# Two of batch 0's key products on GpSimd behind the weights' issues, K in two loads, query products on GpSimd, and a new order list

## The chip, the cores and the metric

The kernel runs on one core of a Trainium2 chip. The metric is the device time of one execution in microseconds. Engines: PE is TensorE (matmuls), DVE is VectorE, ACT is ScalarE, POOL is GpSimd and SP is SyncE, which here issues DMAs only. All times are in microseconds unless ns is written.

## What is computed

A polynomial linear attention, followed by a two-layer feed-forward with SiLU. With 4 batches, 4 heads, 1088 rows and head size 32, r = 8:

```python
def phi(x):                      # 64 features of a row
    a = einsum('rd,bhsd->bhsr', S1, x)
    b = einsum('rd,bhsd->bhsr', S2, x)
    return einsum('bhsi,bhsj->bhsij', a, b).reshape(..., r * r)
q_p, k_p = phi(q), phi(k)
kv  = einsum('bhsf,bhsd->bhfd', k_p, v)
z   = sum(k_p, axis=2)
num = einsum('bhsf,bhfd->bhsd', q_p, kv)
den = einsum('bhsf,bhf->bhs', q_p, z)[..., None] + 1e-06
x   = (num / den).transpose(0, 2, 1, 3).reshape(4352, 128)
h   = x @ w_in                   # 128 x 2048
out = (h * sigmoid(h)) @ w_out   # 2048 x 128
```

## The kernel before, in words

The program is a set of small task functions, and a hand-written list, `ORDER` (lines 19 to 83), that names them one after the other with their arguments. A loop at the end (lines 601 to 604) calls them in that order. Each engine executes its own instructions strictly in the order in which the list recorded them; between engines there are semaphores where data or buffers demand it. So the list decides which instruction stands behind which on each engine, and a wait holds up all that is behind it.

For each batch b the attention goes through these tasks:

- `ld`, `lv` (lines 286 to 291) load K, Q and V. K and Q go through SP's queue, V of batches 1 to 3 through POOL's, which also casts it to bf16. Batch 0's loads stand by themselves at lines 188 to 201: K in four pieces, the second of them issued by ACT, the others by SP.
- `kt`, `qt` (lines 295 and 396): DVE transposes K and Q in blocks of 32.
- `pk` (line 299): PE projects K with the small weights WK into PSUM; `tk` (line 310): DVE transposes the result into the tile `pk` in SBUF. `pc` (line 326) has ACT copy one factor of it into PSUM as well.
- `zs`, `zc`, `mm`, `mk`: the sum of the key features, made into a weight column of WQ with which the denominator comes out of the query projection.
- `kp b e h` (line 319): one of four key products of a batch, 128 x 576 elements, on DVE or (P) on POOL. Where `pc` exists, DVE takes one factor from PSUM.
- `kv` (line 353): PE multiplies the key products with V. Batches 1 to 3 then need `km`, `kr`, `kw`, which mix heads with the constants `E4` and `same`; batch 0 needs only `kw`. The constants are made on POOL by `same_const` (line 270).
- `pq`, `tq`: query projection on PE and its transpose on DVE into `PQ`; `dn` (line 434): four short DVE instructions that apply the denominator (lines 437 to 440); `qo` (line 442): the query product; `pt`: its transpose into `qT`.
- `nm` (line 460): the numerator on PE, and `xc` copies it as bf16 into `xT`, the input of the feed-forward.

The feed-forward runs over 10 chunks of rows (`CHUNKS`), the first of 256, 384 and 448 rows, most others of 512. For each chunk, `f1 c s` makes two or four of the 16 hidden blocks (line 525), `sl c s` is SiLU on ACT (line 533), `f2 c s` adds the block to the output (line 557, or 552 for the last chunks) and `ot c` takes the result out. Three double PSUM banks (slots 0, 1 and 2, the last argument of `f1`, `pk`, `pq` and `nm`) are shared by the hidden blocks and the attention's products, so each must have been read before its slot is written again. The output tile of `f2` has one bank, shared with `zeros`, PE products of ones that are written and never read.

The letters A, V and P in the list choose the engine: ACT, DVE or POOL.

Of the kernel before, what the change touches and what calls it, by code (L numbers as in the profile page):

```python
# [31 lines left out]
dn 0 5 9, f1 1 2 0, tk 1, ld 3, f1 1 1 2, sl 1 0  # L32
lv 1, f2 0 3, f1 1 6 1, sl 1 2, zs 1, sl 1 1
lv 2, qo 0 5 9, sl 1 6, pt 0 5 9, f1 1 3 0, zc 1 V
lv 3, kp 1 1 0 P, sl 1 3, f1 1 5 2, ot 0, mm 1
sl 1 5, f2 1 0, kt 2 0 34, f1 1 7 1, f2 1 1, qt 1 0 34
nm 0 5 9 0, pk 2 2, sl 1 7, mk 1 V, kp 1 0 0 P, kp 1 1 1 P
tk 2, f2 1 2, xc 0 5 9 0 A, kp 1 0 1 P, pq 1 0 9 1 0, f1 2 0 2
kv 1, sl 2 0, tq 1 0 9 0, tq 1 0 9 1, f1 1 4 1, kp 2 1 0 P
f2 1 3, sl 1 4, f1 2 4 2, km 1 V, f1 2 5 0, dn 1 0 4  # L40
qo 1 0 4, f2 1 4, kr 1, kw 1 V, f2 1 5, sl 2 4
f1 2 1 1, pt 1 0 4, f1 2 2 2, sl 2 5, f2 1 6, f2 1 7
ot 1, f1 2 7 0, zs 2, sl 2 1, sl 2 2, dn 1 4 9
nm 1 0 4 1 2, xc 1 0 4 1 V, kt 3 0 34, sl 2 7, qo 1 4 9, f2 2 0
f1 2 3 0, xc 1 0 4 0 A, f2 2 1, f1 2 6 1, f2 2 2, sl 2 3
f1 3 2 2, sl 2 6, pt 1 4 9, f1 3 1 0, zc 2 V, f2 2 3
sl 3 2, f2 2 4, f1 3 0 1, pk 3 2, sl 3 1, tk 3
f1 3 5 0, qt 2 0 34, mm 2, mk 2 V, sl 3 0, f2 2 5
sl 3 5, nm 1 4 9 1 2, xc 1 4 9 0 A, f2 2 6, xc 1 4 9 1 A, f1 3 4 0
f2 2 7, pq 2 0 9 1 2, zs 3, sl 3 4, f1 3 6 0, ot 2  # L50
tq 2 0 9 1, f2 3 0, f1 3 3 2, tq 2 0 9 0, sl 3 6, zc 3 V
f1 4 0 1, dn 2 0 9, kp 2 0 1, sl 3 3, f2 3 1, f1 4 1 0
f2 3 2, qo 2 0 9, sl 4 0, kp 3 1 1 P, kp 2 0 0 P, sl 4 1
kp 2 1 1 P, f1 4 5 2, sl 4 5, f2 3 3, f1 3 7 1, kv 2
sl 3 7, f1 4 7 0, f2 3 4, km 2 V, f1 4 3 2, sl 4 7
f2 3 5, f1 4 6 1, kr 2, f1 4 2 0, pt 2 0 9, kw 2 V
f2 3 6, sl 4 3, sl 4 2, f2 3 7, mm 3, ot 3
mk 3 V, nm 2 0 9 2 0, f2 4 0, sl 4 6, f1 4 4 1, f2 4 1
xc 2 0 9 1 V, qt 3 0 34, xc 2 0 9 0 A, f1 5 0 2, kp 3 0 1, f2 4 2
f1 5 4 0, sl 4 4, f1 5 3 1, f2 4 3, sl 5 0, sl 5 4  # L60
sl 5 3, f2 4 4, pq 3 0 9 2 0, f2 4 5, kp 3 0 0, f1 5 1 1
kp 3 1 0, tq 3 0 9 0, f2 4 6, f1 5 2 2, tq 3 0 9 1, sl 5 1
f2 4 7, ot 4, f1 5 5 0, sl 5 2, sl 5 5, f1 5 6 1
kv 3, f1 5 7 2, f1 6 3 0, f2 5 0, sl 5 6, sl 5 7
f1 6 1 1, dn 3 0 9, f2 5 1, f2 5 2, f2 5 3, f1 6 6 2
km 3 V, sl 6 3, qo 3 0 9, f2 5 4, kr 3, sl 6 1
sl 6 6, f1 6 0 0, pt 3 0 9, f2 5 5, f1 6 2 1, f2 5 6
f2 5 7, sl 6 0, f1 6 4 2, sl 6 2, kw 3 V, ot 5
nm 3 0 9 0 1, f2 6 0, xc 3 0 9 1 V, sl 6 4, f1 6 7 2, f2 6 1
sl 6 7, xc 3 0 9 0 V, f1 6 5 1, f2 6 2, f1 7 1 2, f1 7 0 0  # L70
sl 6 5, f2 6 3, sl 7 1, f2 6 4, sl 7 0, f1 7 6 1
sl 7 6, f1 7 4 2, f2 6 5, f2 6 6, f1 7 3 0, f2 6 7
sl 7 4, sl 7 3, f1 7 2 1, f1 8 2 2, f1 7 5 0, ot 6
f2 7 0, sl 7 2, f2 7 1, f2 7 2, sl 8 2, f1 8 0 1
sl 7 5, f2 7 3, f1 7 7 2, f2 7 4, sl 8 0, f1 8 1 0
sl 7 7, f1 8 3 1, f2 7 5, f2 7 6, f2 7 7, ot 7
sl 8 1, f1 8 4 2, sl 8 3, f1 9 0 0, sl 8 4, f2 8 0
f1 8 5 1, f2 8 1, f1 9 3 2, sl 9 0, sl 8 5, f2 8 2
sl 9 3, f1 8 6 0, f2 8 3, f2 8 4, f1 8 7 1, sl 8 6
f1 9 1 2, f2 8 5, sl 8 7, f2 8 6, sl 9 1, f1 9 2 0  # L80
f1 9 4 1, sl 9 2, f2 8 7, f2 9 0 2, f2 9 1, sl 9 4
ot 8 V, f2 9 2, f2 9 3, f2 9 4, ot 9 V
"""


# [7 lines left out]
def kernel(  # L93
# [188 lines left out]

    def wo():
        nc.gpsimd.dma_start(w_out_bf, moe_w_out.rearrange("(p j) m -> p j m", p=P))
# [25 lines left out]
    def tk(b):  # L310
        t["pk", b] = work.tile([P, NC, 2, 2, 2, R], FP32, name="pk", tag="pk")

        kp_ = work.tile([P, NC * 8 * R * 4], BF16, name="kp", tag="kp")
        t["kp", b] = (kp_.rearrange("p (e n r h j i) -> p e n r h j i", e=2, n=NC, r=2, h=2, j=R) if b in HEADS
                      else kp_.rearrange("p (n r e h j i) -> p e n r h j i", e=2, n=NC, r=2, h=2, j=R))
        t["mark"] = nc.vector.transpose(out=t["pk", b].rearrange("p n r h a i -> p r n (h a i)"),  # L316
                            in_=t["pk_ps", b][:, :, :NC * 32].rearrange("p r (n f) -> p r n f", f=32))

    def kp(b, e, h, eng=nc.vector):
        s = t["pk", b][:, :, :, h].rearrange("p n r a i -> p (n r) a i")  # L320
        o = t["kp", b][:, e, :, :, h].rearrange("p n r j i -> p (n r) j i")
# [1 line left out]
        eng.tensor_tensor(out=o, in0=bcast(s[:, :, 0, 4 * e: 4 * e + 4], 2, R),  # L323
                          in1=bcast(s1, 3, 4), op=ALU.mult)

# [5 lines left out]
    def zs(b):  # L331
        t["z", b] = psA.tile([P, 2 * R], FP32, name="z_ps", tag="ac")
        for n in range(NC):
# [105 lines left out]
        nc.vector.reciprocal(out=dg, in_=dg)  # L439
        nc.vector.tensor_tensor(out=fa, in0=fa, in1=bcast(dg, 2, R), op=ALU.mult)  # L440

    def qo(b, q0, q1):
        fa, fb, fw = feats(b, q0, q1)
        if ("qp", b) not in t:
# [2 lines left out]
        nc.vector.tensor_tensor(out=t["qp", b][:, q0:q1].rearrange("p y h j i -> p (y h) j i"),  # L447
                                in0=bcast(fa, 2, R), in1=bcast(fb, 3, R), op=ALU.mult)
# [186 lines left out]
```

## Time and profile before

| what | value |
|---|---|
| time, three runs | 94.09, 94.91 and 97.61, median 94.91 |
| profiled execution | 93.98, of which 92.3 is the span |
| granted TensorE clock, mean | 0.996 |
| PE busy | 85.9 (93% of the span) |
| DVE busy | 61.3 (66%) |
| ACT busy | 70.6 (77%) |
| POOL busy | 25.0 (27%) |
| first expert product (`f1 0 0`) on PE | 15.39 by the order in time, 15.44 on the chain |

Busy time is the sum over an engine's instructions; the chain of work that ended last is followed backwards from the last instruction, at each step to what released it. A wait is put down to the instruction that came last before it ended.

### The profile page before, as it was taken

To read this page: it belongs to the slowest core of one execution; us is meant where nothing else is said; L and a number is where in the kernel's file an instruction comes from. 1 tells how busy PE (TensorE), PEld (TensorE's weight loads), DVE (VectorE), ACT (ScalarE), POOL (GpSimd) and SP (SyncE) were. 2 spreads that over 40 slices of the span, in tenths; PEclk is the share of its full clock that TensorE was granted. 3 is DMA by queue.
4 is the path that set the end of the run, shared out by engine and by line. 5 is a ranking of instruction groups with operands and counts; after the bars stand their busy time and mean duration, and the time that the engine had idled before them with its cause. 6 is when DMAs were issued, how large, how long until landed. Compare 5 with 4: busy or idle time off the path is not lost.

```text
span 92.3 us, 2484 instructions
## 1 busy us (share of the span) xinstructions
PE 85.9 (93%) x1006; PEld 52.7 (57%) x1006; DVE 61.3 (66%) x109; ACT 70.6 (77%) x88; POOL 25.0 (27%) x66
## 2 busy tenths in 40 slices
...
GB/s 33 248 234 220 158 210 319 321 248 322 269 351 144 5 50 36 7 0 80 26 4 0 60 54 7 11 102 0 0 54 60 7 64 49 0 57 43 7 79 96
DMA packets 20204, 9.31 MB, mean 101 GB/s; under 512 B 16096, under 2 KB 19040, under 8 KB 20192
## 3 DMA queue, kind: packets, MB, share of 16 engines
...
q10 hardware_dynamic: 448, 0.23, 1.0%
q8 instruction: 8, 0.13, 0.6%
...
## 4 chain that ended last, share of the span: by engine, by line
PE 86%; POOL 5%; ACT 3%; DVE 1%; issue 1%; POOLq 0%
PE h_ps L525 33%; PE o_ps L557 27%; PE o_ps L552 6%; PE pk_ps L306 5%; PE zps L249 4%; PE pq_ps L416 2%; ACT g L533 2%; PE kv_ps L365 2%; PE num_ps L476 2%; PE num_ps L467 2%; PE z_ps L337 1%; POOL same L277 1%; PE kv_ps L358 1%; POOL kp L323 1%; DVE pk L316 1%
## 5 line engine op out<-in xcount | busy, mean ns | idle before, releaser
L533 ACT ACTIVATE g<-h_ps 128x1024 bf16<-128x1024 f32 (+3 forms) x73 | 64.2, 1000 | 5.9 <-PE h_ps L525 5.4
L525 PE MATMUL h_ps<-xT,w_in_bf 128*128 128x512 bf16 (+3 forms) x160 | 38.8, 350 | 0.0
L557 PE MATMUL o_ps<-g,w_out_bf 128*128 128x512 bf16 (+3 forms) x128 | 31.9, 353 | 0.2 <-ACT g L533 0.2
L525 PEld LDWEIGHTS <-w_in_bf 128*128 128x128 bf16 x160 | 21.1, 145 | 10.4 <-issue 2.2
L557 PEld LDWEIGHTS <-w_out_bf 128*128 128x128 bf16 x128 | 11.9, 99 | 11.1 <-issue 2.1
L323 POOL TENSOR_TENSOR kp<-pk 128x576 bf16<-128x576 f32 x9 | 10.4, 1183 | 10.6 <-DVE pk L316 10.6
L579 DVE STREAM_TRANSPOSE o_tt<-o_ps 128x512 f32<-128x512 f32 (+3 forms) x8 | 5.2, 644 | 11.9 <-PE o_ps L557 11.9
L447 DVE TENSOR_TENSOR qp<-PQ 128x1024 bf16<-128x1024 f32 (+4 forms) x7 | 10.6, 1515 | 0.1
L296 DVE STREAM_TRANSPOSE KT<-Kx 128x288 f32<-128x288 f32 (+2 forms) x7 | 5.5, 807 | 3.7 <-DMA Kx<-in_k_dram 3.6
L249 PE MATMUL zps<-const-bfloat16-1.0 128*128 128x128 bf16 (+1 forms) x50 | 6.6, 290 | 0.9 <-PEq L619 0.9
L170 POOL DMA_DIRECT2D Vb<-in_v_dram x12 | 6.5, 550 | 3.1 <-DVE qT L454 3.1
L552 PE MATMUL o_ps<-w_out_bf,g 128*128 128x128 bf16 x96 | 6.3, 219 | 0.0
L552 PEld LDWEIGHTS <-g 128*128 128x128 bf16 x96 | 5.9, 98 | 0.6
L235 DVE COPY o_tt<-o_ps 128x512 f32<-128x512 f32 (+1 forms) x2 | 1.0, 492 | 7.8 <-PE o_ps L552 7.8
L398 DVE STREAM_TRANSPOSE QT<-Qx 128x1088 f32<-128x1088 f32 (+3 forms) x6 | 5.4, 910 | 0.4 <-DMA Qx<-in_q_dram 0.4
L249 PEld LDWEIGHTS <-const-bfloat16-1.0 128*128 128x128 bf16 x50 | 4.2, 123 | 2.2 <-issue 2.2
L427 DVE STREAM_TRANSPOSE PQ<-pq_ps 128x576 f32<-128x576 f32 x6 | 4.3, 762 | 1.4 <-PE pq_ps L416 1.4
L306 PE MATMUL pk_ps<-KT,WK 64*32 64x288 f32 x64 | 4.6, 475 | 0.0
L458 DVE STREAM_TRANSPOSE qT<-qp 128x1152 f32<-128x1152 f32 (+2 forms) x4 | 4.3, 1074 | 0.1
L238 ACT ACTIVATE xT<-num_ps 128x256 bf16<-128x256 f32 (+4 forms) x7 | 3.4, 496 | 0.5 <-PE num_ps L467 0.5
L235 DVE CAST xT<-num_ps 128x128 bf16<-128x128 f32 (+3 forms) x10 | 3.4, 459 | 0.5 <-PE num_ps L476 0.5
L238 ACT ACTIVATE KVw<-kv_ps 128x256 bf16<-128x256 f32 x1 | 0.4, 384 | 4.2 <-PE kv_ps L358 4.2
...
## 6 DMA issues: line engine op xcount, KB each, us to landing
...
```

The costliest lines, as they stand in the source:

```text
L170: ins = eng.dma_start(dst, src)
L249: nc.tensor.matmul(t["zps"][:, :ncol], ones[:, :P], ones[:, :ncol], start=True, stop=True)
L296: nc.vector.transpose(out=KT[b % 2][:, y0 * 32: y1 * 32], in_=Kx[b][:, y0:y1, :].rearrange("p a d -> p (a d)"))
L306: nc.tensor.matmul(t["pk_ps", b][32 * c: 32 * (c + 1), r, :NC * 32], w[rs, :], KT[b % 2][rs, c * NC * 32: (c + 1) * NC * 32], start=True, ...
L323: eng.tensor_tensor(out=o, in0=bcast(s[:, :, 0, 4 * e: 4 * e + 4], 2, R), in1=bcast(s1, 3, 4), op=ALU.mult)
L398: nc.vector.transpose(out=QT[b % 2][:, o + y0 * 32: o + y1 * 32], in_=Qx[b][:, y0:y1, :].rearrange("p a d -> p (a d)"))
L447: nc.vector.tensor_tensor(out=t["qp", b][:, q0:q1].rearrange("p y h j i -> p (y h) j i"), in0=bcast(fa, 2, R), in1=bcast(fb, 3, R), op=ALU ...
L525: nc.tensor.matmul(h[:, i, :], w_in_bf[:, j:: NJ], xT[:, t0: t0 + ntok], start=True, stop=True)
L533: nc.scalar.activation(out=gv, in_=t.pop(("h", c, s)), func=ACT.Silu)
L552: nc.tensor.matmul(op[c][:, h, :P] if two else op[c][:, h * P: (h + 1) * P], g[:, i, h * P: (h + 1) * P], w_out_bf[:, j, :], start=(j == 0 ...
L557: nc.tensor.matmul(op[c][:, :ntok], w_out_bf[:, j, :], g[:, i, :], start=(j == 0), stop=(j == NJ - 1))
L579: nc.vector.transpose(out=o_tt[:, :ntok], in_=op[c][:, :ntok])
```

## The change

- K of batch 0 comes in two loads instead of four: rows 0 to 18 by SP, 18 to 34 by ACT. `T2`, a small constant, is issued by SP behind the first rows of Q instead of by ACT.
- `weights` may run on ACT, as two activations, and does.
- The issues of `w_in` and `w_out` on POOL no longer wait for `tk`; they stand directly behind `wq_const` and `weights2`.
- `tk 0` is done in two pieces, and `zs 0` in two as well.
- Two key products of batch 0 (`kp 0 0 1`, `kp 0 1 1`) are on POOL, behind the weights' issues and ahead of `same_const`; the other two stay on DVE, both with `pc`. Before, one was on POOL, behind `same_const`.
- `qo` can run on POOL, and does for the first two blocks of batch 0's Q, and for batches 1, 2 and 3 entirely.
- K and Q of batch 1 come in two halves each.
- The list is written anew: the same products, in another order and with other slots and engines.

The functions:

```diff
-    load_k0(nc.sync, 0)
+    load_kq(nc.sync, 0, k, Kx, 0, 2 * NC)
     nc.scalar.dma_start(T16[R: 2 * R, :], S2)
     nc.sync.dma_start(T16[0:R, :], S1)
-    load_k0(nc.scalar, 1)
-    load_k0(nc.sync, 2)
-    nc.scalar.dma_start(T2, AP(tensor=S2.tensor, offset=S2.offset, ap=[[0, P // R], [D, R], [1, D]]))
-    load_k0(nc.sync, 3)
+    load_kq(nc.scalar, 0, k, Kx, 2 * NC, NY)
     load_kq(nc.sync, 0, q, Qx, 0, 8)
+    nc.sync.dma_start(T2, AP(tensor=S2.tensor, offset=S2.offset, ap=[[0, P // R], [D, R], [1, D]]))
...
-    def weights():
-        nc.vector.tensor_tensor(out=WK.rearrange("p h a i -> p h (a i)"), in0=bcast(t["st"], 1, 2),
-                                in1=bcast(hm2, 2, 2 * R), op=ALU.mult)
+    def weights(copy):
+        w = WK.rearrange("p h a i -> p h (a i)")
+        if copy is acopy:
+            for h in range(2):
+                nc.scalar.activation(out=w[:, h], in_=t["st"], func=ACT.Copy, scale=hm2[:, h: h + 1])
...
     def wi():
-        begin(nc.gpsimd, w_in_bf, moe_w_in, t["mark"])
+        nc.gpsimd.dma_start(w_in_bf, moe_w_in)
...
     def ld(b):
-        load_kq(nc.sync, b, k, Kx, after=t["mark"])
-        load_kq(nc.sync, b, q, Qx)
+        cut = NY // 2 if b == 1 else NY
+        load_kq(nc.sync, b, k, Kx, 0, cut, after=t["mark"])
+        if cut < NY:
+            load_kq(nc.sync, b, k, Kx, cut, NY)
+            load_kq(nc.sync, b, q, Qx, 0, cut)
+        load_kq(nc.sync, b, q, Qx, cut % NY, NY)
...
-        s1 = t["pc", b][:, h] if ("pc", b) in t and eng is nc.vector and e + h else s[:, :, 1]
+        s1 = t["pc", b][:, h] if ("pc", b) in t and eng is nc.vector else s[:, :, 1]
...
-    def qo(b, q0, q1):
+    def qo(b, q0, q1, eng=nc.vector):
...
-        nc.vector.tensor_tensor(out=t["qp", b][:, q0:q1].rearrange("p y h j i -> p (y h) j i"),
+        eng.tensor_tensor(out=t["qp", b][:, q0:q1].rearrange("p y h j i -> p (y h) j i"),
```

The list, cut to what the prediction speaks of; first batch 0's head:

```diff
-zeros 21, turned, kt 0 0 9, weights, wq_const, weights2
-zeros 5, pk 0 0 0 1, kt 0 9 18, kt 0 18 27, kt 0 27 34, pk 0 -1 1 2
-qt 0 0 8, pk 0 -1 2 3, pk 0 -1 3 4, tk 0, wi, wo
-pc 0 1, zeros 17, zs 0, kp 0 0 0, zc 0 V, kp 0 1 1
-zeros 1 512, mm 0, kp 0 1 0, qt 0 8 20, vc0 2 4 A, qt 0 20 34
-mk 0 A, zeros 1 512, pq 0 0 2 2, tq 0 0 2 0, ld 1, dn 0 0 2
-zeros 1 512, pq 0 2 5 0, same_const, vc0 0 2 A, kp 0 0 1 P, qo 0 0 2
-pq 0 5 9 1, kv 0, pt 0 0 2, kw 0 A, tq 0 2 5 0, tq 0 5 9 0
-zeros 2 512, nm 0 0 2 2, xc 0 0 2 0 A, zeros 2 512, f1 0 0 0, f1 0 1 1
-dn 0 2 5, qo 0 2 5, f1 0 2 2, pt 0 2 5, ld 2, sl 0 0
-sl 0 1, f2 0 0, f1 0 3 0, sl 0 2, nm 0 2 5 1, kt 1 0 34
-f2 0 1, pk 1 2, xc 0 2 5 0 A, sl 0 3, f1 1 0 1, f2 0 2
+kt 0 0 9, kt 0 18 27, zeros 22, turned, kt 0 9 18, kt 0 27 34
+weights A, wq_const, weights2, wi, wo, zeros 7
+pk 0 0 0 1, qt 0 0 8, pk 0 -1 1 2, pk 0 -1 2 3, pk 0 -1 3 4, tk 0 0 5
+zeros 13, zs 0 0 5, tk 0 5 9, pc 0 1, zs 0 5 9, zc 0 V
+vc0 2 4 A, zeros 1 512, mm 0, mk 0 A, kp 0 0 0, kp 0 0 1 P
+vc0 0 2 A, qt 0 8 20, zeros 1 512, pq 0 0 2 2, kp 0 1 1 P, kp 0 1 0
+tq 0 0 2 0, dn 0 0 2, qo 0 0 2 P, ld 1, pq 0 2 5 0, qt 0 20 34
+kv 0, zeros 3 512, pq 0 5 9 3, same_const, tq 0 2 5 0, kw 0 V
+lv 1, pt 0 0 2, nm 0 0 2 1, xc 0 0 2 0 A, f1 0 0 2, dn 0 2 5
+sl 0 0, tq 0 5 9 0, f1 0 1 0, qo 0 2 5, pt 0 2 5, ld 2
+f1 0 2 1, dn 0 5 9, f2 0 0, sl 0 1, nm 0 2 5 2, xc 0 2 5 0 V
+f1 0 3 0, sl 0 2, sl 0 3, qo 0 5 9, f2 0 1, kt 1 0 34
+f1 1 1 1, f1 1 3 2, sl 1 1, f2 0 2, lv 2, f1 1 0 0
```

Further on in the new list, from batch 2's `tk` to batch 2's `nm`:

```diff
+tk 2, f1 1 6 0, f2 1 1, sl 1 2, sl 1 6, kp 1 1 0 P
+mm 1, mk 1 V, f1 2 3 2, kp 1 0 1 P, f2 1 2, kp 1 1 1 P
+pq 1 0 9 1 0, zs 2, qt 2 0 34, sl 2 3, tq 1 0 9 0, kp 2 0 1 P
+f1 2 4 2, f2 1 3, f1 2 0 1, tq 1 0 9 1, kp 1 0 0 P, sl 2 4
+zc 2 V, f2 1 4, f1 2 6 0, dn 1 0 4, kv 1, f1 2 2 2
+f2 1 5, sl 2 0, qo 1 0 4 P, sl 2 6, kt 3 0 34, km 1 V
+f2 1 6, f2 1 7, f1 2 7 1, ot 1, kr 1, f1 2 1 0
+kp 2 1 0 P, sl 2 2, sl 2 7, pk 3 2, f1 2 5 1, kp 2 1 1 P
+f2 2 0, kw 1 V, mm 2, pt 1 0 4, tk 3, sl 2 1
+sl 2 5, mk 2 V, dn 1 4 9, nm 1 0 4 0 2, xc 1 0 4 0 A, xc 1 0 4 1 A
+zs 3, pq 2 0 9 1 0, f1 3 2 2, tq 2 0 9 1, f2 2 1, f2 2 2
+tq 2 0 9 0, f1 3 3 0, f2 2 3, qo 1 4 9 P, f1 3 0 1, sl 3 2
+f2 2 4, sl 3 3, sl 3 0, f1 3 7 2, kp 2 0 0, sl 3 7
+f1 3 1 0, f2 2 5, f1 3 4 1, pt 1 4 9, zc 3 V, sl 3 1
+f2 2 6, kv 2, dn 2 0 9, km 2 V, nm 1 4 9 2 0, xc 1 4 9 1 V
+sl 3 4, xc 1 4 9 0 V, f2 2 7, ot 2, kr 2, qo 2 0 9 P
+f1 3 6 1, f1 3 5 0, f1 4 1 2, kw 2 V, sl 3 6, sl 3 5
+f2 3 0, sl 4 1, mm 3, f2 3 1, f1 4 4 1, f2 3 2
+f1 4 0 0, sl 4 4, f1 4 2 2, f2 3 3, kp 3 0 0, f2 3 4
+sl 4 0, sl 4 2, qt 3 0 34, pt 2 0 9, f2 3 5, f1 4 7 1
+f2 3 6, mk 3 V, sl 4 7, nm 2 0 9 0 2, f2 3 7, xc 2 0 9 1 A
```

and around batch 3's query product:

```diff
+f1 5 3 1, f2 4 5, sl 5 0, f2 4 6, f1 5 1 2, f2 4 7
+sl 5 3, kp 3 1 1 P, f1 6 1 0, f1 5 7 1, ot 4, sl 5 1
+kv 3, sl 6 1, km 3 V, qo 3 0 9 P, f2 5 0, f1 5 6 2
+kr 3, f1 6 0 0, kw 3 V, sl 5 7, f2 5 1, f1 5 5 1
+sl 5 6, f2 5 2, pt 3 0 9, f1 6 2 2, sl 6 0, sl 5 5
+f2 5 3, sl 6 2, f2 5 4, nm 3 0 9 0 1, f2 5 5, f1 6 4 2
+xc 3 0 9 0 V, f2 5 6, f1 6 5 0, f2 5 7, sl 6 4, xc 3 0 9 1 V
+f1 6 3 2, ot 5, f1 6 6 1, sl 6 5, f1 7 1 0, sl 6 3
```

More of the change, by code (lines that the diff above doesn't have):

```diff
@@ L29 @@
-dn 0 2 5, qo 0 2 5, f1 0 2 2, pt 0 2 5, ld 2, sl 0 0
-sl 0 1, f2 0 0, f1 0 3 0, sl 0 2, nm 0 2 5 1, kt 1 0 34
-f2 0 1, pk 1 2, xc 0 2 5 0 A, sl 0 3, f1 1 0 1, f2 0 2
[L32 to L82, printed above, removed]
+kt 0 0 9, kt 0 18 27, zeros 22, turned, kt 0 9 18, kt 0 27 34
[4 more added lines that the diff above has]
+vc0 0 2 A, qt 0 8 20, zeros 1 512, pq 0 0 2 2, kp 0 1 1 P, kp 0 1 0
@@ new lines @@
+tq 0 0 2 0, dn 0 0 2, qo 0 0 2 P, ld 1, pq 0 2 5 0, qt 0 20 34
[5 more added lines that the diff above has]
+f1 1 1 1, f1 1 3 2, sl 1 1, f2 0 2, lv 2, f1 1 0 0
+sl 1 3, f1 1 7 1, sl 1 0, f2 0 3, pt 0 5 9, lv 3
+pk 1 2, sl 1 7, nm 0 5 9 0, ot 0, f1 1 4 1, f2 1 0
@@ new lines @@
+tk 1, ld 3, f1 1 2 2, xc 0 5 9 0 A, f1 1 5 0, sl 1 4
+kt 2 0 34, qt 1 0 34, zs 1, pk 2 1, zc 1 V, sl 1 5
+tk 2, f1 1 6 0, f2 1 1, sl 1 2, sl 1 6, kp 1 1 0 P
[6 more added lines that the diff above has]
+kp 2 1 0 P, sl 2 2, sl 2 7, pk 3 2, f1 2 5 1, kp 2 1 1 P
@@ new lines @@
+f2 3 0, sl 4 1, mm 3, f2 3 1, f1 4 4 1, f2 3 2
+f1 4 0 0, sl 4 4, f1 4 2 2, f2 3 3, kp 3 0 0, f2 3 4
+sl 4 0, sl 4 2, qt 3 0 34, pt 2 0 9, f2 3 5, f1 4 7 1
+f2 3 6, mk 3 V, sl 4 7, nm 2 0 9 0 2, f2 3 7, xc 2 0 9 1 A
+f1 4 6 1, xc 2 0 9 0 V, sl 4 6, pq 3 0 9 2 0, ot 3, tq 3 0 9 1
+f2 4 0, f1 4 3 1, sl 4 3, tq 3 0 9 0, f2 4 1, dn 3 0 9
+f1 4 5 0, f1 5 4 2, f1 5 2 1, sl 4 5, kp 3 1 0 P, f2 4 2
+sl 5 2, sl 5 4, kp 3 0 1 P, f2 4 3, f1 5 0 0, f2 4 4
+f1 5 3 1, f2 4 5, sl 5 0, f2 4 6, f1 5 1 2, f2 4 7
@@ new lines @@
+sl 5 3, kp 3 1 1 P, f1 6 1 0, f1 5 7 1, ot 4, sl 5 1
[5 more added lines that the diff above has]
+f1 6 3 2, ot 5, f1 6 6 1, sl 6 5, f1 7 1 0, sl 6 3
+sl 6 6, f2 6 0, f2 6 1, f2 6 2, f1 6 7 2, f2 6 3
+sl 7 1, f1 7 3 1, sl 6 7, f1 7 7 0, sl 7 3, f2 6 4
+f2 6 5, f1 7 0 2, f1 7 2 1, sl 7 7, f2 6 6, sl 7 0
@@ new lines @@
+f2 6 7, sl 7 2, f1 8 2 0, ot 6, sl 8 2, f1 8 0 2
+f1 7 4 1, f2 7 0, sl 8 0, f2 7 1, f1 7 5 0, sl 7 4
+f2 7 2, sl 7 5, f2 7 3, f1 7 6 2, f2 7 4, f1 8 1 1
+sl 7 6, sl 8 1, f2 7 5, f1 8 3 0, f2 7 6, f2 7 7
+f1 8 4 2, f1 8 7 1, sl 8 3, ot 7, f2 8 0, sl 8 4
+f2 8 1, f1 8 6 0, sl 8 7, sl 8 6, f1 8 5 2, f2 8 2
+f1 9 0 1, sl 8 5, f2 8 3, f1 9 1 0, sl 9 0, f2 8 4
+f1 9 3 2, f2 8 5, sl 9 3, f2 8 6, f1 9 2 1, f2 8 7
+sl 9 1, f2 9 0 2, f1 9 4 0, f2 9 1, sl 9 2, f2 9 2
+sl 9 4, ot 8 V, f2 9 3, f2 9 4, ot 9 V
@@ L255, in turned @@
                              tile_position=(0, 32 * i))
-    def weights():
-        nc.vector.tensor_tensor(out=WK.rearrange("p h a i -> p h (a i)"), in0=bcast(t["st"], 1, 2),
-                                in1=bcast(hm2, 2, 2 * R), op=ALU.mult)
+    def weights(copy):
[3 more added lines that the diff above has]
+                nc.scalar.activation(out=w[:, h], in_=t["st"], func=ACT.Copy, scale=hm2[:, h: h + 1])
+        else:
+            nc.vector.tensor_tensor(out=w, in0=bcast(t["st"], 1, 2), in1=bcast(hm2, 2, 2 * R), op=ALU.mult)
     def weights2():
```

24 lines of the change are left out of this document (12 added, 12 removed).

## The prediction

> **What bounds the kernel now.** I read the chain of work that ended last first, since it says which engine set the end of each stretch.
>
> ```profile
> PE 86%; POOL 5%; ACT 3%; DVE 1%; issue 1%; POOLq 0%
> ```
>
> The same chain in order of time (start, length, engine, line) shows the head:
>
> ```profile
> 6.65 0.79 DVE pk L316
> 7.45 0.30 issue
> 7.75 0.74 POOL w_in_bf L170
> 8.49 0.55 POOL w_out_bf L284
> ...
> 11.33 0.31 POOL same L277
> 11.64 1.15 POOL kp L323
> 12.80 0.04 issue
> 12.84 1.18 PE kv_ps L358 x18
> 14.02 0.43 PE zps L249 x2
> 14.46 0.04 issue
> 14.49 0.41 PE num_ps L467 x8
> 14.90 0.54 PE zps L249 x2
> 15.44 0.56 PE h_ps L525 x4
> ```
>
> From 15.44, the first expert product, to 88.36 the chain is almost all PE; its waits there come to about 0.3. So time = first expert product + 72.92 (88.36 - 15.44) + new waits of PE + 3.94 of tail (92.3 - 88.36) + 1.68 outside the span (93.98 - 92.3). Before 15.44 POOL decides: the issue of the two weights, then 2.6 of constants (9.03 to 11.64), then one key product, and only then kv. The sum goes against the profiled 93.98; the median shown, 94.91, lies 0.93 above it, and the lowest run is 94.09.
>
> Second, the waits, for slack of the others.
>
> ```profile
> POOL kp L323 <- DVE pk L316: 10.6, 1, 10.6
> ACT g L533 <- PE h_ps L525: 5.4, 6, 1.6
> ACT KVw L238 <- PE kv_ps L358: 4.2, 1, 4.2
> DVE KT L296 <- DMA Kx<-in_k_dram: 3.6, 2, 3.1
> ```
>
> ACT waits for PE far more than PE for ACT (0.2); POOL has ten idle us in the middle; DVE waits for K at the start. Third, DVE and POOL in order of time at 11 to 13.
>
> ```profile
> 11.61 1.18 POOL L323 TENSOR_TENSOR kp<-pk 128x576 bf16<-128x576 f32 x1
> 11.68 0.20 DVE L439 RECIPROCAL DN<-DN 128x8 f32<-128x8 f32 x1
> 11.91 0.95 DVE L440 TENSOR_TENSOR PQ<-PQ,DN 128x64 f32<-128x64 f32 x1
> ...
> 12.90 0.69 DVE L447 TENSOR_TENSOR qp<-PQ 128x512 bf16<-128x512 f32 x1
> ```
>
> The multiply of L440 has both inputs in SBUF. It took 0.95 and ended as POOL's product ended (12.79); the next one of that line, with half as many elements again, took 0.26 at 15.87 with POOL idle. The reciprocal beside POOL's product was not slowed. This costs the new version more than the old, because POOL gets longer products.
>
> **The change, part by part.**
>
> *K in two loads.* Before, the second transpose of K began at 4.36, when 144 KB issued by ACT at 1.48 had landed, and the last one ended at 5.50. Now ACT's load has 256 KB, and DVE's second transpose waits for it. The 112 KB more, at the 250 GB/s of 2 to 4 us, cost 0.45 alone and 0.9 with half of the rate. Ends 0 (bigger rows may move faster: whole rows moved at over 350 GB/s at 16 us) and 0.9; I take 0.6, since SP's load and q's first rows share the engines. So the last transpose ends at 6.1, pk at 7.2 (1.1 after it, as before), and tk, in two pieces (0.05 more), at 8.1 instead of 7.43.
>
> *Weights on ACT.* Two activations like the 0.17 one that writes WQ, at about 3.75 behind a table load that starts 0.64 earlier because T2's issue leaves ACT. Done at 4.1, before the first K transpose (4.65): nothing. If that cover goes, 0.2. T2 now stands behind q's first rows on SP's queue and lands near 5.5; L4 waits for it on POOL, so w_in issues near 6.05 instead of 7.75 and w_out at 6.8. w_in started moving 1.35 after its issue, so now at 7.4, while q's and v's last loads still move (until 8.8 before). Ends 0 and 1.0 for q's rows 8 to 24 (9.0 before; 1.0 is half the rate over the last us). DVE wants them at 9.3; I take 9.6, so 0.3.
>
> *Key products on POOL.* Two of 1.18 from 8.2 to 10.55, instead of one from 11.61 to 12.79. DVE loses one of 0.76 and runs its two with pc, of 0.75 each, beside them. Whether a product with one input in PSUM is slowed beside POOL no row shows: between 0 and 1.18; I take 0, as for the reciprocal. The Trainium skill, page "SBUF — State Buffer", section "Who interferes with whom", says the same in general: a DVE instruction with two SBUF inputs contends with a GpSimd instruction that reads SBUF, one with at most one SBUF input does not. By that rule the two products with pc cost nothing here and each dn multiply under a POOL product waits; L440's 0.95 against 0.26 agrees.
>
> *DVE's chain then sets the start.* From 8.1: denominators and zt to 8.6, product 9.35, q transpose 9.6 to 10.15 (0.57), product 10.85, PQ 11.2 (0.41), dn's four steps to 12.3 (1.1; they took 11.08 to 12.2 without the block), q transpose 12.85, PQ 13.3, KVw 13.7 (0.39), qT 14.1 (0.45). kv runs 11.1 to 12.3 and POOL's first query product 12.3 to 13.35 (512 elements x 2.05 ns, by 1183/576), both under it. Then num 0.41, xT 0.38 and gaps: first expert product at 15.05. Gain 0.39.
>
> *What moves behind it.* POOL's constants, 2.6, now follow that query product: 13.4 to 16.0, then v's loads. POOL's loads use eight completion slots in turn, so batch 3's v (its eleventh to fourteenth load) waits for batch 1's (third to sixth) to land, as it does before: issued 16.0, landed 5.5 to 7.2 later, before the issue at about 20.4. Ends 0 and 2.8 on POOL. The five key products then take 5.75 and end between 29.0 and 31; PE reaches kv of batch 1 near 30.3 in the new list. I take 0.2 of PE wait (0 to 1).
>
> *xT of rows 256 to 640* goes from ACT (0.51) to DVE, behind the dn of the last part (1.2 from 17.3): 18.5 to 19.05. PE, which filled this with pk before, has only its own last products there: 0.35.
>
> *Query products on POOL.* Batch 1: 2.1 and 2.6 instead of 1.2 and 1.45; batches 2 and 3: 4.7 (2304 x 2.05) instead of 2.55. By page "GPSIMD Engine Reference", section 3.1 "Elementwise", 2048 elements take 4497 ns, which would be 5.06 for 2304, an estimate 0.35 above; the row decides. DVE is relieved of 7.75, but km of batch 1 stands behind dn and K3's transpose there (0.3, ends 0 and 0.6), nm 1 behind tk 3 (0.15). Batch 2's product, from 42.7 to 47.4, blocks kp 3 0 0 on DVE from about 45; behind it stand Q3's transpose (1.3) and qT (1.37), so nm 2 starts at 50.4 to 50.8 against PE's arrival at 50.2: 0.4 (0 to 1). Batch 3's ends near 60.7, four us before its num: nothing.
>
> Sum: -0.39 + 0.2 + 0.35 + 0.3 + 0.15 + 0.4 = +1.0: 93.98 + 1.0 = 95.0. ACT's xT copies fall by 0.8, hidden: it waits for PE 5.4.
>
> **Rivals.**
> *The head's gain stays.* If ACT's K load lands at 4.4 and q is not late, the first expert product comes at about 14.45 (-1.0); with waits of 0.2 the time is 93.2. For it: POOL is wholly out of the head's chain. Against: DVE then carries 6.9 us in a row, and its list puts work ahead of xT, km and qT.
> *POOL's query products set the end (slower).* The four take 11.5 against 6.65 on DVE, and while one runs, DVE's two-input multiplies stand still. Place: batches 1 and 2, pt behind qo. It decides once PE arrives at nm 1 or nm 2 more than 0.4 before qT. Were half of the 4.85 uncovered, beside my other waits of 0.6, it gives 93.98 + 2.4 + 0.6 = 97.0. For it: L440. Against: POOL's 10 idle us, and PE has expert products to do.
> *v's loads hold the key products.* Batch 3's v waits the full 2.8: kv 1 waits 1 more, km and qo 1 slide behind it by 0.4: 96.4. For it: batches 2 and 3 landed in 7.1 to 8.8. Against: batch 1 landed in 5.5 to 6.0.
>
> **How the numbers follow.** 95.0 has 0.47 (its own range 94.2 to 95.9), the kept gain 0.23, POOL's query products 0.17, v's loads 0.13. About 2% is what a measurement of this kernel can tell from no change: below 93.0 or above 96.8 against 94.91. Faster by over 2%: the better half of the kept gain, 0.10. Slower: two thirds of POOL's case, a third of the loads' and some of what I have not thought of, 0.20. Within: 0.70. Range 93.0 to 97.2: it leaves out the best of the kept gain, 0.10, and the worst of the slow cases, 0.10.
>
> **What the new profile would show.** tk ending near 8.1 and not 7.43 if K is late; POOL's two products from 8.2; first expert product near 15.05; kv with no wait for POOL; DVE's products with pc at 0.75 beside POOL's (1.9 would refute that); POOL's 2304 product at 4.7, and kp 3 0 0 stretched beside it; PE idle ahead of the first chunk-1 product, of kr 1 and of nm 2. I am wrong if the first expert product comes before 14.6 and PE stays full (the kept gain), or if PE stands idle more than 2 us behind 15 (slower).

## The result, and the profile after

| | before | after |
|---|---|---|
| median on the first chip | 94.57 (94.09 to 97.61, 4 runs) | 95.64 (95.17 to 95.77, 4 runs) |
| ratio on the first chip | | 1.0145, interval 1.0109 to 1.018 |
| ratio on another chip, more runs | | 1.0095, interval 1.0062 to 1.0129 |
| profiled execution, span | 93.98, 92.3 | 95.17, 93.5 |
| PE, DVE, ACT, POOL busy | 85.9, 61.3, 70.6, 25.0 | 86.2, 55.8, 70.5, 43.1 |

The ratios leave out executions that took over 1.5% more than the fastest of the same kernel, as the 97.61 of before. The changed kernel is about 1% slower, inside what was called no change. By stretch, in the profiled executions (start of the first expert product on the chain, end of PE's last product, end of the span):

| stretch | before | after | difference |
|---|---|---|---|
| start to first expert product | 15.44 | 15.22 | -0.22 |
| from there to PE's last end (88.36, 89.91) | 72.92 | 74.69 | +1.77 |
| tail to the end of the span | 3.94 | 3.59 | -0.35 |
| outside the span | 1.68 | 1.67 | 0 |

The chain of work that ended last, by engine:

```profile
PE 76%; DVE 14%; DMA 3%; ACT 2%; issue 1%; SPq 0%
```

POOL has left it (5% before) and DVE has come in (1% before). The same chain in order of time (start, length, engine, tile, line):

```profile
0.82 0.41 SPq L170
1.23 0.06 issue
1.28 2.53 DMA T<-in_S_dram
...
4.25 0.86 PE zps L244 x7
5.11 1.78 PE pk_ps L309 x16
6.89 1.50 PE zps L244 x13
8.39 0.65 PE z_ps L342 x36
9.05 0.54 PE zps L244
...
13.45 1.06 PE pq_o L412 x8
14.79 0.39 ACT xT L233
15.22 0.61 PE h_ps L530 x4
...
27.78 1.45 DVE PQ L432 x2
...
29.29 1.93 DVE AW L442
...
32.07 1.30 DVE KT L299
33.37 0.32 DVE km L384
...
45.53 2.69 DVE kp L327
```

Three things are to be seen. First, the head does not hang on POOL any more, nor on DVE: it starts with a transfer of 1 KB (`T`, the constant S1), and then PE's own filler products (`zps`) and sums (`z_ps`) make up the chain. Second, at 27.78 to 33.37 the chain runs through DVE, with a multiply of line 442 that takes 1.93. Third, at 45.53 a key product on DVE (`kp 3 0 0`) takes 2.69 on the chain, 2.77 in DVE's own record, beside POOL's query product.

The waits:

```profile
ACT g L538 <- PE h_ps L530: 7.3, 11, 1.2
DVE KT L299 <- DMA Kx<-in_k_dram: 4.0, 2, 3.7
POOL Vb L170 <- DMA Vb<-in_v_dram: 1.9, 2, 1.3
PE kv_ps L370 <- POOL kp L327: 1.1, 1, 1.1
PE st_ps L249 <- DMA T<-in_S_dram: 0.6, 1, 0.6
PE num_ps L481 <- DVE WQ L230: 0.2, 1, 0.2
PE kr_ps L390 <- DVE km L384: 0.2, 1, 0.2
```

POOL's single wait of 10.6 for DVE, which ended at 38.70 before, is gone: its query products stand in that stretch now. PE, which behind the head hardly waited before, now waits 1.1 for POOL's key products of batch 1, and the line above shows what POOL had waited for: V's loads. POOL in order of time:

```profile
7.87 2.31 POOL L327 TENSOR_TENSOR kp<-pk 128x576 bf16<-128x576 f32 x2 [0.64 <-DVE pk L320]
12.68 1.07 POOL L452 TENSOR_TENSOR qp<-PQ 128x512 bf16<-128x512 f32 x1 [2.51 <-DVE PQ L445]
...
16.87 4.93 POOL L170 DMA_DIRECT2D Vb<-in_v_dram  x9
22.37 0.55 POOL L170 DMA_DIRECT2D Vb<-in_v_dram  x1 [0.57 <-DMA Vb<-in_v_dram]
24.22 1.09 POOL L170 DMA_DIRECT2D Vb<-in_v_dram  x2 [1.30 <-DMA Vb<-in_v_dram]
25.33 5.72 POOL L327 TENSOR_TENSOR kp<-pk 128x576 bf16<-128x576 f32 x5
...
43.45 4.16 POOL L452 TENSOR_TENSOR qp<-PQ 128x2304 bf16<-128x2304 f32 x1 [3.30 <-DVE PQ L445]
```

The nine issues at 16.87 end with the first of batch 3's four loads of V; the other three are issued at 22.37 to 25.31, after 0.57 and 1.30 of waiting. In the trace the second waits on the semaphore that told of batch 1's second load (landed at 22.09), the third on that of batch 1's third (23.94): these are the completion slots that the prediction spoke of. The five key products start only behind them. On DVE:

```profile
9.19 0.74 DVE L327 TENSOR_TENSOR kp<-pk,pc_ps 128x576 bf16<-128x576 f32 x1
10.34 0.71 DVE L327 TENSOR_TENSOR kp<-pk,pc_ps 128x576 bf16<-128x576 f32 x1
...
29.26 1.94 DVE L442 TENSOR_TENSOR AW<-PQ 128x128 f32<-128x128 f32 x1
```

The product with one factor in PSUM (`pc_ps`) takes 0.74 while POOL's own products run at 7.87 to 10.18, and the second one, behind them, 0.71; the multiply with both inputs in SBUF takes 1.94 beside POOL's, against 0.29 without them (experiment a).

### The profile page after: what moved, and what is told of

It reads as the page before. It is cut to its first block, busy times and chain, and to the rows that moved or that the text cites. A ratio compares the mean times of both kernels' runs of the same rounds, so it can differ in the third digit from the quotient of the medians.

```text
span 93.5 us, 2483 instructions
## 1 busy us (share of the span) xinstructions
PE 86.2 (92%) x1003; PEld 53.8 (58%) x1003; DVE 55.8 (60%) x104; ACT 70.5 (75%) x87; POOL 43.1 (46%) x74
## 4 chain that ended last, share of the span: by engine, by line
PE 76%; DVE 14%; DMA 3%; ACT 2%; issue 1%; SPq 0%
PE h_ps L530 27%; PE o_ps L562 21%; PE o_ps L557 6%; PE zps L244 4%; PE pk_ps L309 4%; DVE kp L327 3%; DMA T<-in_S_dram 3%; PE pq_ps L421 3%; PE num_ps L481 2%; DVE AW L442 2%; PE z_ps L342 2%; DVE PQ L432 2%; DVE KT L299 1%; DVE qT L463 1%; PE num_ps L472 1%; DVE QT L403 1%
## 5 line engine op out<-in xcount | busy, mean ns | idle before, releaser
L452 POOL TENSOR_TENSOR qp<-PQ 128x2304 bf16<-128x2304 f32 (+3 forms) x5 | 13.7, 2743 | 13.4 <-DVE PQ L445 13.4
L562 PEld LDWEIGHTS <-w_out_bf 128*128 128x128 bf16 x128 | 12.1, 98 | 10.6 <-issue 0.9
L327 POOL TENSOR_TENSOR kp<-pk 128x576 bf16<-128x576 f32 x12 | 14.3, 1220 | 0.7 <-DVE pk L320 0.6
L230 DVE CAST xT<-num_ps 128x128 bf16<-128x128 f32 (+5 forms) x12 | 4.5, 473 | 2.8 <-PE num_ps L481 2.6
L244 PEld LDWEIGHTS <-const-bfloat16-1.0 128*128 128x128 bf16 x47 | 4.9, 144 | 1.9 <-issue 1.7
L233 ACT ACTIVATE xT<-num_ps 128x256 bf16<-128x256 f32 (+2 forms) x5 | 2.2, 457 | 4.3 <-PE num_ps L472 4.3
L327 DVE TENSOR_TENSOR kp<-pk 128x576 bf16<-128x576 f32 x2 | 4.3, 2154 | 0.0
L309 PE MATMUL pk_ps<-KT,WK 64*32 64x288 f32 x64 | 4.0, 481 | 0.1
## 6 DMA issues: line engine op xcount, KB each, us to landing
w_out_bf<-in_moe_w_out_dram POOLq DMA_DIRECT2D x1, 512.0 KB, 10.1
```

Source lines behind the costliest of these rows:

```text
L244: nc.tensor.matmul(t["zps"][:, :ncol], ones[:, :P], ones[:, :ncol], start=True, stop=True)
L309: nc.tensor.matmul(t["pk_ps", b][32 * c: 32 * (c + 1), r, :NC * 32], w[rs, :], KT[b % 2][rs, c * NC * 32: (c + 1) * NC * 32], start=True, ...
L452: eng.tensor_tensor(out=t["qp", b][:, q0:q1].rearrange("p y h j i -> p (y h) j i"), in0=bcast(fa, 2, R), in1=bcast(fb, 3, R), op=ALU.mult)
L562: nc.tensor.matmul(op[c][:, :ntok], w_out_bf[:, j, :], g[:, i, :], start=(j == 0), stop=(j == NJ - 1))
```

## The experiments

Theory going in: V's loads of batch 3, issued ahead of the key products on POOL, cost the time behind 15, and the late 1 KB of S1 costs the head its gain. Rivals: POOL's longer query products, K in two loads, and a limit elsewhere. The runs come in four groups, each with fresh executions of before to compare with. In the first group before took 94.59.

**a_lv3_late.** Batch 3's V is issued later on POOL, behind batch 1's second query product:

```diff
-sl 1 3, f1 1 7 1, sl 1 0, f2 0 3, pt 0 5 9, lv 3
+sl 1 3, f1 1 7 1, sl 1 0, f2 0 3, pt 0 5 9
...
-tq 2 0 9 0, f1 3 3 0, f2 2 3, qo 1 4 9 P, f1 3 0 1, sl 3 2
+tq 2 0 9 0, f1 3 3 0, f2 2 3, qo 1 4 9 P, lv 3, f1 3 0 1, sl 3 2
```

> The new kernel, with only batch 3's v loads moved on POOL from ahead of the key products of batch 1 to behind the second query product of batch 1. Theory (v's completion slots hold the key products): POOL waited 1.87 us for slots and spent about 1.65 us on issuing, so its first key product of batch 1 starts at about 23.1 instead of 25.33, the fifth ends near 28.9 instead of 31.05, PE's wait of 1.05 at kv 1 and of 0.16 at kr 1 go, and the time falls by 1.0 to 1.3. Rival (the chain of DVE and POOL behind batch 1 sets the end, not kv 1): the wait comes back at nm 1 or nm 2 and the time falls by less than 0.4.

Measured: 93.84 (93.25 to 94.25), ratio to before 0.99 (0.9863 to 0.9936). This one move turns 1% slower into 1% faster, more than the 1.0 to 1.3 us expected. POOL, DVE and PE in order of time:

```profile
23.70 5.74 POOL L327 TENSOR_TENSOR kp<-pk 128x576 bf16<-128x576 f32 x5 [2.13 <-DVE pk L320]
```
```profile
29.81 0.29 DVE L442 TENSOR_TENSOR AW<-PQ 128x128 f32<-128x128 f32 x1
```
```profile
17.70 0.61 PE L562 MATMUL o_ps<-g,w_out_bf 128*128 128x256 bf16 x4 [0.67 <-DMA w_out_bf<-in_moe_w_out_dram]
...
30.44 0.69 PE L370 MATMUL kv_ps<-Vb,kp 128*128 128x64 bf16 x18
```

The five products start 1.63 earlier and end at 29.44, ahead of line 442, which is back at 0.29; kv of batch 1 waits for nothing. Where the same PE instruction starts in both tells what each wait was worth: after is 0.56 ahead of a at the product in front of kv 1 (29.51 against 30.07), 0.66 behind it at kv 1 (31.10 against 30.44) and 0.99 behind it at kr 1 (33.73 against 32.74). So V's loads cost 1.22 at kv 1 and 0.33 at kr 1. From the first output product to PE's last end it is 71.3 in before, 73.0 in after and 71.1 in a: without V's loads the new list loses nothing there. What the theory had not seen is the last fence's first line: PE waits 0.67 for `w_out`.

**b_s1_first.** S1's load is put ahead of K's first on SP's queue:

```diff
+    nc.sync.dma_start(T16[0:R, :], S1)
     load_kq(nc.sync, 0, k, Kx, 0, 2 * NC)
...
-    nc.sync.dma_start(T16[0:R, :], S1)
```

> The new kernel, with only the 1 KB load of S1 issued on SP ahead of K's first load instead of behind it. Theory (the bigger first load of K held S1 back, PE stood idle 0.58 and then ran its head at half pace): the small transposed weights come at about 3.4 instead of 3.94, the projection of K ends near 6.7 instead of 6.89, the 13 zeros products take about 0.9 instead of 1.57, and the first expert product comes at 14.3 to 14.7 instead of 15.22; the time falls by 0.4 to 0.8. Rival (DVE's own chain sets the start): the first expert product moves by 0.2 or less and the time by 0.2 or less.

Measured: 96.2 (95.72 to 96.64), ratio 1.0168 (1.012 to 1.0216), no better than after. S1 came in time (the product that reads it starts at 3.30, without a wait), but K's first transpose began at 4.65 instead of 3.65, so PE's gap only moved: 0.81 ahead of pk, and the first expert product came at 15.71. The expectation failed: the price of this order is a K that is 1.0 later. Part of the time is V's loads again, for which kv 1 waited 1.53 here and 1.05 in after.

**c_qo_dve.** The query products of batches 1 to 3 go back to DVE:

```diff
-f2 1 5, sl 2 0, qo 1 0 4 P, sl 2 6, kt 3 0 34, km 1 V
+f2 1 5, sl 2 0, qo 1 0 4, sl 2 6, kt 3 0 34, km 1 V
...
-kv 3, sl 6 1, km 3 V, qo 3 0 9 P, f2 5 0, f1 5 6 2
+kv 3, sl 6 1, km 3 V, qo 3 0 9, f2 5 0, f1 5 6 2
```

(and `qo 1 4 9` and `qo 2 0 9` alike).

> The new kernel, with the query products of batches 1, 2 and 3 back on DVE (those of batch 0 as they are). Theory (they cost PE little where they stand, about 0.2 at nm 2): DVE's kp 3 0 0 takes 0.75 instead of 2.77, PE's waits at kv 1 stay, and the time changes by less than 0.5 either way. Rival (POOL's long products and the port are what the change loses): the time falls by 0.8 or more.

Measured: 104.02 (102.63 to 105.6), ratio 1.0915 (1.0844 to 1.0987). No theory had this. POOL and DVE in order of time, and PE's granted clock by slices of 2.6:

```profile
25.70 7.99 POOL L327 TENSOR_TENSOR kp<-pk 128x576 bf16<-128x576 f32 x7
```
```profile
29.14 4.70 DVE L442 TENSOR_TENSOR AW<-PQ 128x128 f32<-128x128 f32 x1
```
```profile
PEclk9999999999999955599999999999999999999997
```

With no query product among them, POOL's seven key products run back to back for 7.99, and DVE's multiply, started at 29.14, ends at 33.84, with the last of them (33.69). km 1 and everything behind it is late, PE stands idle 3.69 ahead of kr 1, and from the 15th to the 17th slice (35.8 to 43.4) its granted clock is about half. So taking the query products off POOL saves nothing in this list: POOL's wait for DVE ahead of the first of them (1.18 in after) is what let DVE's multiply in. What they cost by themselves c does not tell, since it takes that break away too.

**d_k_four.** K in four loads and T2 issued by ACT, as before:

```diff
-    load_kq(nc.sync, 0, k, Kx, 0, 2 * NC)
+    load_kq(nc.sync, 0, k, Kx, 0, NC)
...
-    load_kq(nc.scalar, 0, k, Kx, 2 * NC, NY)
+    load_kq(nc.scalar, 0, k, Kx, NC, 2 * NC)
+    load_kq(nc.sync, 0, k, Kx, 2 * NC, 3 * NC)
...
```

> The new kernel, with batch 0's K again in four loads, with T2 again issued by ACT, as in the kernel before; all else as it is. Theory (two big loads held S1 back): S1 lands near 3.2, PE's head runs at full pace again, and the first expert product comes 0.3 to 0.7 earlier than 15.22; the time falls by as much. Rival (the two loads cost nothing, DVE sets the start): 0.2 or less. My prediction had put the cost on K's own landing, 0.6 later; if that were so, the last K transpose would end earlier than the 5.58 of the new kernel.

Measured: 95.85 (94.49 to 98.02), ratio 1.0075 (1.0028 to 1.0122). The interval overlaps that of after, so the time tells nothing. Its profiled execution took 98.02, the longest of the twelve, and only the head is read from it: S1 in time (3.29), the 13 fillers in 0.94 and the sums from 7.71 in 0.50, against 1.57 and, from 8.32, 0.72 in after. Its last K transpose ended at 6.09, not earlier than the 5.58 of after.

In the second group before took 94.57. **after_again** is the changed kernel once more.

> The new kernel unchanged, on the same chip as the next three, so that they can be compared: 95.4 to 95.8, PE's wait at kv 1 near 1.0. If the five key products of batch 1 start before 24.5 here, the wait at kv 1 is shorter and the time lower by the same amount.

Measured: 95.46 (95.15 to 96.79), ratio 1.0095 (1.0062 to 1.0129). In its profile POOL waits 2.8 for V's slots and kv 1 waits 1.81 for POOL, more than the 1.9 and 1.1 of the first; that execution took 96.41. The wait is this kernel's own, and its size depends on when V lands.

**e_zeros5.** As a, with 5 filler products instead of 13 ahead of the sums (the fillers' results are never read):

```diff
-zeros 13, zs 0 0 5, tk 0 5 9, pc 0 1, zs 0 5 9, zc 0 V
+zeros 5, zs 0 0 5, tk 0 5 9, pc 0 1, zs 0 5 9, zc 0 V
```

> The new kernel with batch 3's v loads late (as in the run a_lv3_late), and 5 instead of 13 zeros products between the projection of K and the sums of the key features. Theory (the 13 products take 1.5 to 1.6 at half pace, where DVE and POOL already wait for the sums): the sums begin 0.6 to 0.9 earlier and the first expert product 0.4 to 0.7 earlier than in a_lv3_late; the time falls by as much, unless w_out, which landed between 16.8 and 17.7, holds the first output product back. Rival (PE needs that work to come to full pace): the products behind stay slow (a 512-column product at 0.6 instead of 0.39 past 10 us), and the first expert product gains less than 0.2.

Measured: 93.16 (93.04 to 93.69), ratio 0.9869 (0.9829 to 0.9908). The first expert product comes at 14.24, 1.31 earlier than in a. Of this, 0.46 is not the edit's: the projection of K ended at 7.34 in a and at 6.88 here. The rest, 0.85, is about what the eight fillers took (1.57 less 0.71), so the head did hang on PE's own fillers. But the ratio moves only from 0.99 to 0.9869, within the intervals:

```profile
17.07 0.61 PE L562 MATMUL o_ps<-g,w_out_bf 128*128 128x256 bf16 x4 [1.36 <-DMA w_out_bf<-in_moe_w_out_dram]
```

Half of the gain (0.69) is given back at the next wait: the first output product, which waits 1.36 for `w_out` instead of a's 0.67.

**f_kp3_behind.** As a, with `kp 3 0 0` behind `pt 2 0 9` on DVE, so that it does not start beside POOL's query product:

```diff
-f1 4 0 0, sl 4 4, f1 4 2 2, f2 3 3, kp 3 0 0, f2 3 4
-sl 4 0, sl 4 2, qt 3 0 34, pt 2 0 9, f2 3 5, f1 4 7 1
+f1 4 0 0, sl 4 4, f1 4 2 2, f2 3 3, f2 3 4
+sl 4 0, sl 4 2, qt 3 0 34, pt 2 0 9, kp 3 0 0, f2 3 5, f1 4 7 1
```

> The new kernel with batch 3's v loads late (as in a_lv3_late), and batch 3's first key product on DVE moved behind the transpose of batch 2's query product, so that it no longer stands on DVE beside POOL's long query product. Theory (its stretch from 0.75 to 2.65 is hidden but for 0.2 at nm 2): the stretch is gone, and the time falls by 0 to 0.3. Rival (the port is where the change loses): the time falls by 0.8 or more.

Measured: 93.45 (92.88 to 94.08), ratio 0.9892 (0.9845 to 0.9939), the same as a's within the intervals. The stretch was real (2.65 in a; 1.55 here, where it stands beside POOL's key products) and hidden: nm 2 starts at 49.66 in a and at 49.60 here.

**g_before_const_late.** The kernel before, with its key product ahead of the constants on POOL, the one part of the change that the prediction saw as the head's gain:

```diff
-zeros 1 512, pq 0 2 5 0, same_const, vc0 0 2 A, kp 0 0 1 P, qo 0 0 2
+zeros 1 512, pq 0 2 5 0, vc0 0 2 A, kp 0 0 1 P, same_const, qo 0 0 2
```

> The kernel before, with one thing of the change alone: POOL's key product of batch 0 ahead of the 2.6 us of constants instead of behind them. Theory (in the kernel before, POOL's constants set the start of kv and so of everything): kv starts near 12.0 instead of 12.84, DVE's dn multiply is not stretched, the first expert product comes near 14.4 instead of 15.42, and the time falls by 0.6 to 1.1 against the kernel before. Rival (w_out, which landed at 16.1, or the chain behind sets the pace): the first expert product comes earlier, but the time falls by less than 0.3.

Measured: 94.22 (93.15 to 94.9), ratio 0.9949 (0.9917 to 0.998). The first expert product comes at 14.74 instead of 15.39, 0.65 earlier, and only about 0.35 of that arrives in the medians (94.57 to 94.22). In the profiled execution none is left at the first output product, which starts at 17.27 and at 17.10 in before:

```profile
17.27 0.61 PE L557 MATMUL o_ps<-g,w_out_bf 128*128 128x256 bf16 x4 [1.06 <-DMA w_out_bf<-in_moe_w_out_dram]
```

`w_out`, issued at 8.5 in both, landed at 17.23 here and at 16.12 in before. So the old kernel meets the same limit behind its head when `w_out` lands late.

In the third group before took 94.54. **h_ld1_late** is e with batch 1's K and Q issued later (`ld 1` from behind `qo 0 0 2 P` to behind `pt 0 0 2`), to clear the way for `w_out`.

> The kernel of e_zeros5, with batch 1's K and Q held until the transpose of batch 0's first query product (about 13.3) instead of the first PQ (about 10.5). Theory (w_out, issued at 6.7, shares the transfers with them and lands at 16.8 to 17.8, which holds the first output product and takes back the head's gain): w_out lands at 15 to 16.3, PE's wait of 1.36 for it falls below 0.6, and the time falls by 0.5 to 1.0 against e_zeros5, to about 92.4. Rival (w_out is slow by itself, or K of batch 1 comes too late for its transpose near 19): w_out still lands past 16.6, or the wait comes back at the projection of batch 1's K, and the time falls by less than 0.2.

Measured: 93.87 (92.96 to 95.03), ratio 0.9885 (0.9842 to 0.9929): no gain over e. The wait for `w_out` falls from 1.36 to 0.46, but K of batch 2, behind batch 1's on the queue, is now late (DVE waits 0.53 for it at 22.87, and PE 0.43 ahead of its projection at 24.33). The gain went to the next wait.

**j_zeros27.** As a, with 27 fillers instead of 22 at the very start, so that PE does not stand idle until S1 lands:

```diff
-kt 0 0 9, kt 0 18 27, zeros 22, turned, kt 0 9 18, kt 0 27 34
+kt 0 0 9, kt 0 18 27, zeros 27, turned, kt 0 9 18, kt 0 27 34
```

> The kernel of a_lv3_late, with 27 instead of 22 zeros products at the very start, so that PE is busy until S1's load lands (3.8 to 3.9) instead of standing idle 0.4 to 0.6 there. Theory (that gap is why PE's head stays at half pace until about 9): the 13 products behind K's projection take about 0.95 as in the kernel before (17 in 1.17) instead of 1.57, the key sums 0.50 instead of 0.70, and the first expert product comes 0.4 to 0.8 earlier than 15.55. Rival (the pace hangs on something else): the 13 products still take 1.5 or more and nothing moves by more than 0.2.

Measured: 93.27 (92.86 to 95.17), ratio 0.9854 (0.9808 to 0.99). PE's head in j, and in after:

```profile
0.86 3.04 PE L244 MATMUL zps<-const-bfloat16-1.0 128*128 128x128 bf16 x27 [0.86 <-PEq L624]
...
6.54 1.06 PE L309 MATMUL pk_ps<-KT,WK 64*32 64x288 f32 x12 [0.96 <-DVE KT L299]
7.54 0.94 PE L244 MATMUL zps<-const-bfloat16-1.0 128*128 128x128 bf16 x13
8.40 0.50 PE L342 MATMUL z_ps<-pk 128*32 128x16 f32 x36
```
```profile
3.94 0.30 PE L249 MATMUL st_ps<-I,T 16*32 16x16 f32 x8 [0.58 <-DMA T<-in_S_dram]
...
6.83 1.57 PE L244 MATMUL zps<-const-bfloat16-1.0 128*128 128x128 bf16 x13
8.32 0.72 PE L342 MATMUL z_ps<-pk 128*32 128x16 f32 x36
...
9.83 0.59 PE L244 MATMUL zps<-const-bfloat16-1.0 128*128 128x512 bf16 x1
```

The same 13 fillers take 1.57 in after (0.121 each) and 0.94 in j (0.072 each), and the same 36 sums 0.72 and 0.50. Without the gap of 0.58 at 3.4, PE runs faster from 7.5 on. The other traces agree: with a gap of 0.39 to 0.60 there (after, its repeat, a, c, e, f, h) the full pace first shows between 7.5 and 10.4, without it (before, d, g, j, k, l) always by 7.6. Although K's second load landed late in this execution (the wait of 0.96), the first expert product came at 14.98, against a's 15.55. In time the gain is not clear of a's (0.9854 and 0.99, with intervals that overlap). A gap of 0.96 at 5.6 did not bring the slow pace back here, nor did one of 0.74 at 5.1 in d; so it is the place of the gap, and not its length alone, that counts.

In the fourth group before took 94.35. **k_all** is a, e, f and j together.

> The new kernel with batch 3's v loads late, batch 3's first key product behind the transpose, 27 zeros products at the start and 5 instead of 13 behind the projection of K. If the gains add, the first expert product comes near 14.0 and the time is 92.3 to 92.8, 2% under the kernel before. If w_out (15.6 to 17.8) holds the first output product, as in the run e_zeros5, it stays at 93.0 to 93.5.

Measured: 93.07 (92.58 to 96.05), ratio 0.9842 (0.9796 to 0.9887). The first expert product comes at 13.95 and the span is 91.0. It is faster than both kernels, but its interval overlaps those of e and j, so the gains did not add. What holds it is again

```profile
16.27 0.61 PE L562 MATMUL o_ps<-g,w_out_bf 128*128 128x256 bf16 x4 [0.85 <-DMA w_out_bf<-in_moe_w_out_dram]
```

**l_all_ld1** is k_all with `ld 1` issued later, as in h.

> The kernel of k_all, with batch 1's K and Q also held as in h_ld1_late. If what holds k_all is w_out's landing, this is 0.3 to 0.8 faster than k_all; if the wait returns at the projection of batch 2's K, as in h_ld1_late, it is within 0.2 of it.

Measured: 93.33 (92.99 to 93.91), ratio 0.9894 (0.9854 to 0.9934), not better than k_all. PE now waits 0.65 for `w_in` and 0.97 for `w_out`, which landed 10.0 after its issue, no earlier than in after (10.1). What makes the weights land late stays open: keeping batch 1's loads away did not help reliably, and no run issued the weights over another queue.

## Why the prediction was right, and where its steps were not

The forecast of 95.0 stands against 95.17 in the profiled execution and a median of 95.64. The direction and the size of the sum were right, in part by luck: the term that turned out largest, V's loads, was put at 0.2, and other terms came out smaller.

*Key products on POOL behind the weights' issues: right.* POOL's two products ran at 7.87 to 10.18 (forecast 8.2 to 10.55) and left the chain; DVE's first with `pc` took 0.74 beside them (forecast 0.75), against 0.71 for the second, which began when they were done. That agrees with the Trainium skill, page "SBUF — State Buffer", section "Who interferes with whom", by which such an instruction, with at most one SBUF input, does not contend with GpSimd.

*K in two loads, +0.6 on K's landing: wrong mechanism.* The last K transpose ended at 5.58 against 5.50 before, so 0.08. What was late was something the prediction passed over: S1's 1 KB, which stands behind K's first load on SP's queue, now twice as large, landed at 3.81. Before, the product that reads it started at 3.31; now PE stood idle 0.58 ahead of it and then ran slowly through its fillers and sums. The error is in "DVE's chain then sets the start": DVE's tk ended at 7.78, earlier than the forecast 8.1, and then DVE itself waited 1.31 for the sums (until 9.09). The step "denominators and zt to 8.6" left 0.5 behind tk for them; it took 1.48 (7.78 to 9.26), since the 13 fillers stand ahead of the sums on PE. PE set the start. That the start came out near the forecast (15.22 against 15.05) is luck: the sums came later than forecast, while K came 0.52 earlier (5.58 against 6.1) and DVE did not wait for Q (forecast until 9.6). e and j show that PE's head was the limit, with 14.24 and 14.98.

*V's loads: right place, wrong size.* The term was 0.2, with 0 to 1 as bounds. It measured 1.22 at kv 1 by a, and 1.81 of wait in the repeat. The forecast had the key products end between 29.0 and 31 and PE arrive at 30.3; they ended at 31.05 and PE was there at 29.88 (31.10 less 1.22). They were at the late end because POOL waited 1.87 for V's slots (2.8 in the repeat; the bounds named were 0 to 2.8), and because batch 1's V was issued from 16.87 and not 16.0: the constants took 3.2 instead of 2.6, one of their selects 0.88 beside a DVE product, against 0.31 for others. This is the rival with 0.13, "v's loads hold the key products"; it happened, while the total stayed near the forecast since the next terms were smaller. In the repeat, with the full 2.8, the profiled execution took 96.41, which is that rival's figure (96.4), though the median of the repeat's ten is 95.46.

*xT on DVE, +0.35:* about 0.19, by the same reckoning against a (0.79 ahead at the product before it, 0.60 at the one that reads xT). *km and kr behind dn, +0.3:* 0.33, but not for the reason given: in a, with the same order on DVE, kr 1 waits for nothing. It was line 442, stretched from 0.29 to 1.94 by the late key products of POOL, so it belongs to V's loads. *nm 1, +0.15:* no wait. *nm 2, +0.4:* 0.17, with kp 3 0 0 at 2.77 as forecast in kind.

*Query products on POOL: right, and a little dear.* 1.07, 1.95, 2.39 and 4.16 for 512, 1024, 1280 and 2304 elements, against 1.05, 2.1, 2.6 and 4.7; the longer ones cost 1.8 to 1.9 ns an element and not the 2.05 taken from the 576 of a key product. The estimate of 5.06 by the Trainium skill, page "GPSIMD Engine Reference", section 3.1, is further from 4.16; the measurement decides. The rival that they set the end is refuted: PE has no wait for them but the 0.17 ahead of nm 2, and a, which leaves them all on POOL, is faster than before. Its sum was wrong besides: the prediction's own figures for the four add to 14.1 on POOL and 7.75 on DVE, not 11.5 and 6.65, and would have made it 97.8; measured were 12.65 on POOL.

*The kept head gain (93.2):* e and g say why it could not come whole: `w_out` takes back 0.69 of the 1.31 by which e's head is shorter, and all of the 0.65 in g's profiled execution. The issue of the two weights 1.8 earlier brought `w_out` in at 16.8 against 16.1 before, later and not earlier; no step of the prediction had the landing of the weights as a limit.

Sum as measured: -0.22 + 0.19 + 1.22 + 0.33 + 0.17 - 0.35 = 1.34, against 1.19; the rest, -0.15, is not assigned. The -0.35 of the tail is no effect of the change: g, whose list ends as before's does, has a tail of 3.59 against before's 3.94. So it too is luck.
